# Moving the third transform stage's nine VectorE copies to ScalarE in a fused FFT and two-MLP kernel

## The chip, the cores and the metric

One core of one Trainium2 chip runs the kernel. The metric is the device time of an execution in microseconds (us). Engines are named as in the profile: PE is TensorE's matmul, DVE is VectorE, ACT is ScalarE, POOL is GpSimd, SP is SyncE, which here only issues DMAs.

## What is computed

The reference takes the real part of a two-dimensional FFT of x (2 batches, 3008 rows, 256 features) and sends the 6016 resulting rows through two gated MLPs.

```python
X = np.fft.fft(x, axis=1)
X = np.fft.fft(X, axis=2)
x = X.real.reshape(6016, 256)
gate = 1.0 / (1.0 + np.exp(-(x @ w_gate)))      # 256 -> 1536
x = gate * (x @ w_val) @ w_out                  # 1536 -> 256
h = x @ w_in                                    # 256 -> 2048
out = (h * np.cos(h)) @ w_out2                  # 2048 -> 256
```

The weights arrive as 64-bit floats, and the kernel itself turns them into 32-bit ones.

## The kernel before

The transform over 3008 rows is split into factors 47 and 64, and the one over features is a 128-row cosine or sine matrix. So there are three matmul stages. The first (L325, 16 chunks) writes D1. The second (`stage_b`, L375, 12 calls named b00 to b15) reads D1 and is stored as a rounded high part D2h (ACT, L401) and a remainder D2l (DVE, L405). The third (`stage_c`, L410, six calls c00 to c12, one for each tile of 502 columns) gives three PSUM results a call. These are E (even part), one extra row of features, and O (odd part), and they are copied into the tile's SBUF buffer eo0 to eo5. These 18 copies are the ones in question (L427 on DVE, L430 on ACT). A token is E + O, and its mirror image is E - O.

The first MLP has 6 x 12 = 72 steps (`step1`, L601): one tile by one 128-wide slice of the hidden layer. PE multiplies E into PSUM banks 4 and 5 (`ab(s, 0)`, L475 to L477) and O into banks 6 and 7 (`ab(s, 1)`). DVE adds the extra feature row (`even`, L493, two instructions) and then forms E + O and E - O (`tokens`, L501, two instructions). `ab(s+1, 0)` may not overwrite banks 4 and 5 before L493 of step s has read them, and `ab(s+1, 1)` not banks 6 and 7 before L501 of step s. ACT applies the sigmoid (L649), POOL multiplies gate and value (L505), ACT makes the rounded product and its negative (L589, L590), POOL starts a DMA that adds the exact product onto that negative (L528), and four steps later PE multiplies by the output weights (`out1`, L515 to L518). The second MLP (L539 on) follows.

Beside this, 39 weight units run through a fixed list of steps (`unit_steps`, L139): a DMA into a free buffer, decoding of the 64-bit pattern by two ACT instructions (L118, L119), three DVE instructions (L122, L124, L126) and one POOL instruction (L129), then for most units a rounding on ACT (L134) and a remainder on DVE or POOL (L135); a unit of the first MLP's input weights also has an add and a subtract on DVE or POOL (L150, L151). Their order is fixed when the program is built. The list `clk` holds a planned time for each engine. `regular` (L218) plans a fixed instruction, after `fill` (L196) has placed unit steps that should end before it; `spend` adds its planned length. A step that DVE or POOL may run goes where the planned time is lower. Units whose buffers will be overwritten by the first MLP's own tiles are driven to their end, whatever the planned time, by a loop (L643, L644) that stands just ahead of `tokens(s)` at L646. Each engine then runs its instructions in this order, waiting on semaphores.

The third stage and the first MLP overlap: c10, b15, `ab(0, 0)`, `ab(0, 1)`, c11, `ab(1, 0)`, c12, `ab(1, 1)` is the order on PE. A copy's engine is chosen in `evac` (L421) from the planned times alone.

Of the kernel before, what the change touches and what calls it, by code (L numbers as in the profile page):

```python
# [49 lines left out]
def fft_moe_moe(ctx: ExitStack, tc: tile.TileContext, x, x0, head, w1, w1s, wo1, w2, t1, t3, out):  # L50
# [10 lines left out]
    V, A, G, PE = nc.vector, nc.scalar, nc.gpsimd, nc.tensor  # L61
# [41 lines left out]
    clk = {V: 0.0, A: 0.0, G: 0.0, DQ: 0.0}  # L103
    VG = (V, G)

    def spend(e, us, after=0.0):
        clk[e] = max(clk[e], after) + us
        return clk[e]
# [87 lines left out]
    def fill(e, until):  # L196

        while True:
            for un in live:
                step = un[2][0]  # L200
                if step[0] is VG and e is G and max(un[3], clk[V]) + VADV < max(un[3], clk[G]):
                    continue
                if e in step[0] if step[0] is VG else e is step[0]:
                    if max(un[3], clk[e]) + cost(step, e) <= until:
                        step_of(un, e)
                        break
            else:
                if e is DQ and len(todo) > held[0] and clk[e] + 1.5 <= until:
                    for bf in free:
                        if bf[2] <= until and max(clk[e], bf[2]) + LIFE <= bf[1]:  # L210
                            start(bf)
                            break
                    else:
                        return
                    continue
                return

    def regular(e, us, at=0.0):  # L218

        fill(e, at)  # L220
        return spend(e, us, at)

    def finish(un):
        while un in live:
            step_of(un)
# [46 lines left out]
    def slot(t, us, ahead):  # L272
        while after:
            after.pop(0)()
        for _ in range(2):
            for e, k in zip((DQ, A, G, V), ahead):
                fill(e, t + us + k)
# [93 lines left out]
    def bank():  # L371
        nbank[0] = (nbank[0] + 1) % nbank[1]
        return nbank[0]
# [36 lines left out]
    def stage_c(b, ch, ahead=AHB):  # L410
        slot(now, 2.54, ahead)
        t = b * NCH + ch
        sl = slice(ch * PC, (ch + 1) * PC)
        h0, h1, l0, l1 = D2h[:, 0, sl], D2h[:, 1, sl], D2l[:, 0, sl], D2l[:, 1, sl]

        def mm(terms, dst):
            o = ps[:, bank(), 0:PC]
            for i, (w, m) in enumerate(terms):
                PE.matmul(o, w, m, start=(i == 0), stop=(i == len(terms) - 1))

            def evac(at=now + 2.54):  # L421
                for un in list(live):
                    if un[1] and un[1][0] is flat[t]:
                        finish(un)
                if clk[V] + .59 < clk[A] + .2:
                    regular(V, .59, at)
                    V.tensor_copy(dst, o)  # L427
                else:
                    regular(A, .47, at)
                    A.copy(dst, o)  # L430

            after.append(evac)


        mm([(T3h[:, 0], h0), (T3h[:, 0], l0), (T3l[:, 0], h0), (T3h[:, 2], h1), (T3h[:, 2], l1)],
           eo[t][:, 0, 0:PC])
        mm([(T3h[:, 3], h0), (T3h[:, 3], l0), (T3h[:, 4], h1), (T3h[:, 4], l1)],
           eo[t][:, 0, PC:TW])
        mm([(T3h[:, 1], h1), (T3h[:, 1], l1), (T3l[:, 1], h1)],
           eo[t][:, 1, 0:PC])  # L440
        return now + 2.54
# [364 lines left out]
```

## Time and profile before

| what | value |
|---|---|
| median of 3 runs | 1040.05 us (1039.76 to 1040.32) |
| profiled execution, its own time | 1041.4 us |
| its span, first to last instruction | 1039.5 us |
| mean granted TensorE clock | 0.986 |
| PE busy | 1005.1 us |
| DVE busy | 780.4 us |
| ACT busy | 765.0 us |
| POOL busy | 668.0 us |

A row of a timeline has the start, the length, engine, line, operation, what is written and read, how many instructions are merged, and in brackets the idle time of that engine before it with what ended it. Lengths overlap by some hundredths where the next instruction is started early. The granted clock is the share of full speed, so 0.50 is 1.2 GHz and 1.00 is 2.4 GHz.

### The profile page before, as it was taken

The numbers are of one execution on the slowest core, as the hardware profiler recorded it, in microseconds if no ns is written. First come the engines' busy times: TensorE is split into PE (matmuls) and PEld (weight loads), VectorE is DVE, ScalarE is ACT, GpSimd is POOL, SyncE is SP. The second block draws the span as 40 slices with busy tenths as digits, with TensorE's granted clock in tenths as the row PEclk, the third lists the DMA queues.
The fourth block names the chain that finished last, engine by engine and source line by source line (L and its number), as shares of the span: only waits on it lengthen the run. The fifth ranks groups of instructions, "written<-read, shape, count | busy, mean of one in ns | idle before, by whom it ended". The sixth has DMA issues, their size and how long they took to land.

```text
span 1039.5 us, 13150 instructions
## 1 busy us (share of the span) xinstructions
PE 1005.1 (97%) x4566; PEld 838.0 (81%) x4566; DVE 780.4 (75%) x1033; ACT 765.0 (74%) x1207; POOL 668.0 (64%) x521
## 2 busy tenths in 40 slices
PE   8788899999898999999999999999999999999998
PEld 8776688788786888888788888888888888888886
DVE  3699888877778777777576777777777777777775
ACT  3765566667465567575698888988888888888886
POOL 2685887777676777777365656656566465665753
PEclk9999899999898999999999999999999999999999
DMA  9731556665565566688700000000000000000000
GB/s 255 216 102 41 110 130 140 161 141 124 146 150 121 129 151 146 150 226 211 191 1 20 1 21 0 21 21 1 20 1 21 20 1 21 0 20 21 1 20 21
DMA packets 25955, 85.59 MB, mean 82 GB/s; under 512 B 3168, under 2 KB 6560, under 8 KB 25888
## 3 DMA queue, kind: packets, MB, share of 16 engines
q0 software_dynamic: 10368, 37.02, 19.0%
q1 hardware_dynamic: 15296, 47.59, 14.0%
q8 instruction: 36, 0.59, 0.2%
q14 instruction: 31, 0.25, 0.1%
q10 hardware_dynamic: 224, 0.14, 0.0%
HBM read 33.16 MB, written 14.56 MB: 46 GB/s over the span
## 4 chain that ended last, share of the span: by engine, by line
PE 73%; DVE 4%; ACT 2%; DMA 1%; issue 1%; POOL 0%; DVEq 0%; ACTq 0%
PE ps L557 25%; PE ps L475 12%; PE ps L476 12%; PE ps L477 12%; PE ps L515 4%; PE ps L517 4%; PE ps L518 4%; DVE D L501 3%; DMA gh<-D 1%; ACT gh L589 1%; DVE D L124 1%; DVE D L122 1%; ACT gh L590 1%; DVE D L493 0%; ACT eo L524 0%
## 5 line engine op out<-in xcount | busy, mean ns | idle before, releaser
L583 POOL TENSOR_TENSOR h<-D,h 128x502 fp32r<-128x502 f32 x191 | 284.3, 1489 | 215.8 <-ACT h L582 204.1
L557 PE MATMUL ps<-h,wr 128*128 128x502 f32 x1152 | 291.9, 389 | 0.0
L475 PE MATMUL ps<-es,wr 128*128 128x502 f32 x672 | 265.6, 395 | 16.1 <-DVE D L501 10.9
L476 PE MATMUL ps<-es,wr 128*128 128x502 f32 x672 | 264.3, 393 | 0.0
L477 PE MATMUL ps<-es,wr 128*128 128x502 f32 x672 | 263.3, 392 | 0.0
L557 PEld LDWEIGHTS ps<-h,wr 128*128 128x128 f32 x1152 | 217.8, 189 | 44.4
L505 POOL TENSOR_TENSOR D<-D 128x502 f32<-128x502 f32 x144 | 186.3, 1352 | 93.0 <-ACT D L649 93.0
L568 DVE SCALAR_TENSOR_TENSOR D<-D,ps 128x502 f32<-128x502 int32 x192 | 130.2, 678 | 117.8 <-POOL h L583 110.0
L501 DVE TENSOR_TENSOR D<-D,ps 128x1004 f32<-128x1004 f32 x144 | 172.9, 1201 | 51.6 <-PE ps L477 30.0
L649 ACT ACTIVATE D<-D 128x1004 f32<-128x1004 f32 x72 | 75.1, 1044 | 149.8 <-DVE D L501 149.8
L475 PEld LDWEIGHTS ps<-es,wr 128*128 128x128 f32 x672 | 127.6, 190 | 46.5 <-DVE D L501 13.7
L569 DVE SCALAR_TENSOR_TENSOR D<-D 128x502 f32<-128x502 int32 x192 | 144.8, 754 | 6.6
L477 PEld LDWEIGHTS ps<-es,wr 128*128 128x128 f32 x672 | 127.8, 190 | 26.6
L476 PEld LDWEIGHTS ps<-es,wr 128*128 128x128 f32 x672 | 127.9, 190 | 25.5
L567 ACT ACTIVATE D<-ps 128x502 int32<-128x502 f32 x192 | 113.0, 589 | 47.3 <-PE ps L477 45.4
L575 DVE TENSOR_TENSOR D<-D,ps 128x502 f32<-128x502 f32 x192 | 128.9, 672 | 16.1 <-ACT D L574 16.1
L573 ACT ACTIVATE D<-D 128x502 f32<-128x502 f32 x192 | 119.2, 621 | 12.2 <-DVE D L569 9.7
L493 DVE SCALAR_TENSOR_TENSOR D<-eo,w,ps 128x502 f32<-128x502 f32 x144 | 101.8, 736 | 32.7 <-PE ps L477 32.3
L574 ACT ACTIVATE D<-D 128x502 f32<-128x502 f32 x192 | 120.0, 625 | 6.1
L582 ACT CAST h<-D 128x502 fp32r<-128x502 f32 x192 | 114.6, 597 | 0.2 <-DVE D L575 0.2
L517 PE MATMUL ps<-gh,wr 128*128 128x502 f32 x288 | 114.3, 397 | 0.0
L518 PE MATMUL ps<-gh,wr 128*128 128x502 f32 x288 | 113.4, 394 | 0.0
(86 smaller groups left out, 1073.7 us busy)
## 6 DMA issues: line engine op xcount, KB each, us to landing
gh<-D POOLq DMA_DIRECT2D x72, 502.0 KB, 4.7
D<-in_w_dram SPq DMA_DIRECT2D x17, 512.0 KB, 4.3
ws<-D SPq DMA_DIRECT2D x16, 512.0 KB, 3.6
wr<-ws SPq DMA_DIRECT2D x16, 512.0 KB, 4.0
out_dram<-D SPq DMA_DIRECT2D x24, 251.0 KB, 2.9
raw<-in_x_dram SPq DMA_DIRECT2D x15, 384.0 KB, 9.6
eo<-in_w_dram SPq DMA_DIRECT2D x11, 512.0 KB, 10.3
D<-in_wo_dram SPq DMA_DIRECT2D x6, 512.0 KB, 4.9
```

The costliest lines, as they stand in the source:

```text
L475: PE.matmul(o, w_hi, m_hi, start=first, stop=False)
L476: PE.matmul(o, w_lo, m_hi, start=False, stop=False)
L477: PE.matmul(o, w_hi, m_lo, start=False, stop=last)
L501: V.tensor_tensor(out=gv[s][:, :, c:c + PC], in0=sas, in1=ps[:, 6:8, 0:PC], op=op)
L505: G.tensor_tensor(out=gv[p][:, 1, m], in0=gv[p][:, 1, m], in1=gv[p][:, 0, m], op=ALU.mult)
L517: PE.matmul(o, WO1[:, f, 0, m], h[:, 0, sl], start=(f == 0), stop=False)
L518: PE.matmul(o, WO1[:, f, 1, m], h[:, 0, sl], start=False, stop=False)
L557: PE.matmul(o, WO2[:, f, i, d * 128:(d + 1) * 128], h[:, m], start=(f == 0 and i == m == 0), stop=(f == NF2 - 1 and m == 1))
L568: V.scalar_tensor_tensor(out=r, in0=k, scalar=-C1, in1=h, op0=ALU.mult, op1=ALU.add)
L569: V.scalar_tensor_tensor(out=r, in0=k, scalar=-C2, in1=r, op0=ALU.mult, op1=ALU.add)
L575: V.tensor_tensor(out=r, in0=r, in1=ps[:, 4 + s % 4, 0:PC], op=ALU.mult)
L583: (V if s == N2S - 1 else G).tensor_tensor(out=h[:, 1], in0=r, in1=f32(h[:, 0]), op=ALU.subtract)
```

## The change

All 18 copies are made by ACT, and the planned time of DVE is no longer charged for nine of them.

```diff
@@ stage_c, evac
-                if clk[V] + .59 < clk[A] + .2:
-                    regular(V, .59, at)
-                    V.tensor_copy(dst, o)
-                else:
-                    regular(A, .47, at)
-                    A.copy(dst, o)
+                regular(A, .47, at)
+                A.copy(dst, o)
```

The change shortens the file by four lines, so from there on every line number is four lower in the changed kernel: L493 is L489 there, L501 is L497, L505 is L501, L528 is L524, L589 is L585, L590 is L586, L649 is L645; lines up to L425 keep theirs. As planned times decide the order, steps of weight units move too. D_73 is the buffer of weight units and of the first MLP's tiles, gh the rounded products, wr the finished weights.

POOL from the decoding ahead of the first step's products on. Before:

```order
L129 TENSOR_TENSOR D_73<-D_73 128x512 x2
L505 TENSOR_TENSOR D_73<-D_73 128x502 x2
L528 DMA gh_771<-D_73 128x1004
L505 TENSOR_TENSOR D_73<-D_73 128x502 x4
L528 DMA gh_801<-D_73 128x1004
L505 TENSOR_TENSOR D_73<-D_73 128x502 x2
L528 DMA gh_825<-D_73 128x1004
L135 TENSOR_TENSOR es_770<-eo_66,es_770 128x502
L505 TENSOR_TENSOR D_73<-D_73 128x502 x2
```

and with the change:

```order
L129 TENSOR_TENSOR D_73<-D_73 128x512
L501 TENSOR_TENSOR D_73<-D_73 128x502 x2
L524 DMA gh_769<-D_73 128x1004
L501 TENSOR_TENSOR D_73<-D_73 128x502 x2
L129 TENSOR_TENSOR D_73<-D_73 128x512
L501 TENSOR_TENSOR D_73<-D_73 128x502 x2
L524 DMA gh_802<-D_73 128x1004
L501 TENSOR_TENSOR D_73<-D_73 128x502 x2
L524 DMA gh_826<-D_73 128x1004
L129 TENSOR_TENSOR D_73<-D_73 128x512
L135 TENSOR_TENSOR es_768<-eo_66,es_768 128x502
L501 TENSOR_TENSOR D_73<-D_73 128x502 x2
```

The second of the two L129 that stood together, which belongs to the third output-weight unit, has moved behind the products of step 0, the first product DMA and the products of step 1. Behind the third product DMA there is now an L129 ahead of the next tile's L135 (es).

ACT from the rounding of the second output-weight unit to the second step's product. Before:

```order
L134 CAST wr<-D_73 128x2x256 x2
L118 ACTIVATE D_73<-D_73 128x512
L119 ACTIVATE D_73<-D_73 128x512
L649 ACTIVATE D_73<-D_73 128x1004
L430 COPY eo_70<-ps 128x502
L589 CAST gh_771<-D_73 128x1004
L590 ACTIVATE gh_771<-D_73 128x1004
L649 ACTIVATE D_73<-D_73 128x1004
L589 CAST gh_801<-D_73 128x1004
```

and with the change:

```order
L134 CAST wr<-D_73 128x2x256
L118 ACTIVATE D_73<-D_73 128x512
L119 ACTIVATE D_73<-D_73 128x512
L118 ACTIVATE D_73<-D_73 128x512
L119 ACTIVATE D_73<-D_73 128x512
L645 ACTIVATE D_73<-D_73 128x1004
L426 COPY eo_70<-ps 128x502 x3
L585 CAST gh_769<-D_73 128x1004
L586 ACTIVATE gh_769<-D_73 128x1004
L134 CAST wr<-D_73 128x2x256
L645 ACTIVATE D_73<-D_73 128x1004
L585 CAST gh_802<-D_73 128x1004
```

The sigmoid shown first in each piece is that of step 1. The two L134 of before round the second and the third output-weight unit; the third unit's now stands behind that sigmoid, the three copies of the last tile (one before), and the product pair of step 0.

DVE from the remainder of the third output-weight unit (L135) to `tokens` of step 5. Before:

```order
L135 TENSOR_TENSOR wr<-D_73,wr 128x2x256
L501 TENSOR_TENSOR D_73<-D_73,ps 128x2x502 x2
L493 SCALAR_TENSOR_TENSOR D_73<-eo_65,w_71,ps 128x502 x2
L122 TENSOR_SCALAR D_73<-D_73 128x512
L501 TENSOR_TENSOR D_73<-D_73,ps 128x2x502 x2
L493 SCALAR_TENSOR_TENSOR D_73<-eo_65,w_71,ps 128x502 x2
L124 TENSOR_SCALAR D_73<-D_73 128x512
L501 TENSOR_TENSOR D_73<-D_73,ps 128x2x502 x2
L126 SCALAR_TENSOR_TENSOR D_73<-D_73 128x512
L493 SCALAR_TENSOR_TENSOR D_73<-eo_65,w_71,ps 128x502 x2
L122 TENSOR_SCALAR D_73<-D_73 128x512
L501 TENSOR_TENSOR D_73<-D_73,ps 128x2x502 x2
```

and with the change:

```order
L135 TENSOR_TENSOR wr<-D_73,wr 128x2x256
L497 TENSOR_TENSOR D_73<-D_73,ps 128x2x502 x2
L489 SCALAR_TENSOR_TENSOR D_73<-eo_65,w_71,ps 128x502 x2
L124 TENSOR_SCALAR D_73<-D_73 128x512
L497 TENSOR_TENSOR D_73<-D_73,ps 128x2x502 x2
L489 SCALAR_TENSOR_TENSOR D_73<-eo_65,w_71,ps 128x502 x2
L126 SCALAR_TENSOR_TENSOR D_73<-D_73 128x512
L497 TENSOR_TENSOR D_73<-D_73,ps 128x2x502 x2
L122 TENSOR_SCALAR D_73<-D_73 128x512
L489 SCALAR_TENSOR_TENSOR D_73<-eo_65,w_71,ps 128x502 x2
L124 TENSOR_SCALAR D_73<-D_73 128x512
L497 TENSOR_TENSOR D_73<-D_73,ps 128x2x502 x2
```

The same L135 stands ahead of `tokens(2)`; the decoding steps L122, L124, L126 of the next units have moved, and an L122 now stands right behind `tokens(4)` and ahead of `even(5)`. The matmuls of PE and the DMAs of SP stand in the same order in both kernels.

## Rows read from the trace of the kernel before

**Rows 1.** Waits of PE, whole span: who waited for whom, us in total, times, longest.

```profile
PE ps L475 <- DVE D L501: 10.9, 6, 4.2
```

**Rows 2.** Windows: busy us (instructions) of PE, PEld, DVE, ACT, POOL; granted clock; DMA.

```profile
60.00:92.00 32.00, 27.38 (x159) 23.57 (x158) 31.73 (x49) 19.76 (x44) 27.18 (x22) 0.95 0.15 55
```

**Rows 3.** One line's instructions, L427 and L430: shortest, median, longest ns.

```profile
L427 DVE COPY eo<-ps x9: 664/671/674, 61.3 to 99.5; 128x502 f32<-128x502 f32 x9
...
L430 ACT COPY eo<-ps x9: 552/572/592, 60.2 to 99.9; 128x502 f32<-128x502 f32 x9
```

**Rows 4.** Timeline of DVE from tokens(1) to tokens(3).

```profile
96.51 2.44 DVE L501 TENSOR_TENSOR D<-D,ps 128x1004 f32<-128x1004 f32 x2 [1.41 <-PE ps L477]
...
101.34 0.68 DVE L135 TENSOR_TENSOR wr<-D,wr 128x512 fp32r<-128x512 f32 x1
101.94 2.43 DVE L501 TENSOR_TENSOR D<-D,ps 128x1004 f32<-128x1004 f32 x2
104.47 1.38 DVE L493 SCALAR_TENSOR_TENSOR D<-eo,w,ps 128x502 f32<-128x502 f32 x2
105.77 3.42 DVE L122 TENSOR_SCALAR D<-D 128x512 f32<-128x512 f32 x1
109.11 2.42 DVE L501 TENSOR_TENSOR D<-D,ps 128x1004 f32<-128x1004 f32 x2
```

**Rows 5.** Timeline of ACT: two copies; later the sigmoid of step 1, a product pair.

```profile
66.27 1.02 ACT L430 COPY eo<-ps 128x502 f32<-128x502 f32 x2
...
98.98 1.04 ACT L649 ACTIVATE D<-D 128x1004 f32<-128x1004 f32 x1 [3.62 <-DVE D L501]
...
100.39 1.03 ACT L589 CAST gh<-D 128x1004 fp32r<-128x1004 f32 x1
101.32 1.04 ACT L590 ACTIVATE gh<-D 128x1004 fp32r<-128x1004 f32 x1
```

**Rows 6.** Timeline of POOL: product DMA, four products, a decoding step.

```profile
102.95 1.00 POOL L528 DMA_DIRECT2D gh<-D  x1 [6.72 <-PE ps L477]
103.69 5.21 POOL L505 TENSOR_TENSOR D<-D 128x502 f32<-128x502 f32 x4
...
121.62 1.60 POOL L129 TENSOR_TENSOR D<-D 128x512 int32<-128x512 int32 x1
```

**Rows 7.** Timeline of DVE around 72, 196 and 259 us.

```profile
72.36 1.73 DVE L126 SCALAR_TENSOR_TENSOR D<-D 128x512 uint32<-128x512 uint32 x1
...
195.86 4.58 DVE L124 TENSOR_SCALAR D<-D 128x512 uint32<-128x512 uint32 x1
...
258.61 5.37 DVE L124 TENSOR_SCALAR D<-D 128x512 uint32<-128x512 uint32 x1
```

**Rows 8.** Timeline of POOL around 72 and 259 us.

```profile
72.26 1.28 POOL L135 TENSOR_TENSOR wr<-eo,wr 128x512 fp32r<-128x512 f32 x1 [1.06 <-ACT wr L134]
...
257.62 1.19 POOL L528 DMA_DIRECT2D gh<-D  x1
258.22 1.70 POOL L135 TENSOR_TENSOR es<-eo,es 128x502 fp32r<-128x502 f32 x1
...
260.73 2.87 POOL L505 TENSOR_TENSOR D<-D 128x502 f32<-128x502 f32 x2
```

**Rows 9.** Timeline of PE: the matmuls that waited after the long L124 of 196 and 259 us.

```profile
201.14 0.50 PE L475 MATMUL ps<-es,wr 128*128 128x502 f32 x1 [0.80 <-DVE D L493]
...
204.31 0.50 PE L475 MATMUL ps<-es,wr 128*128 128x502 f32 x1 [1.54 <-DVE D L501]
...
264.68 0.50 PE L475 MATMUL ps<-es,wr 128*128 128x502 f32 x1 [1.34 <-DVE D L493]
...
267.96 0.79 PE L475 MATMUL ps<-es,wr 128*128 128x502 f32 x1 [1.66 <-DVE D L501]
```

**Rows 10.** Windows: two stretches at a granted clock of 0.50, columns as in rows 2.

```profile
109.98:116.81 6.83, 5.22 (x13) 4.18 (x14) 6.30 (x7) 3.40 (x4) 4.05 (x4) 0.50 0.40 78
266.99:273.82 6.83, 5.86 (x14) 4.73 (x15) 5.22 (x6) 3.31 (x4) 4.62 (x4) 0.50 0.45 120
```

## The prediction

> **What bounds the kernel now.** I read the page first, then the waits of PE, then the timelines of all engines from 60 to 140 us, then windows. PE is busy nearly throughout, so only what makes PE wait, or run at half clock, counts. Its largest wait is for L501, `tokens`, on DVE: 10.9 us in six places [rows 1]. The copies in question lie between 60 and 100 us. There DVE is busy 31.73 of 32 us, POOL 27.18, ACT only 19.76 [rows 2]. So DVE looks like the engine to relieve and ACT like the one with room, which speaks for the change. But the order pieces show that more than nine copies moves, and the prediction rests on where three other instructions land.
>
> The reader is to see in [rows 4] that in this part PE follows DVE: `tokens(1)` ends at 98.95, `tokens(2)` starts at 101.94 and `tokens(3)` at 109.11, and each releases PE. The last was late because an L122 took 3.42 us. Such a decoding step is short when POOL is idle, and long when it meets a run of POOL instructions behind a product DMA. The L124 of 258.61 lasted 5.37 us, to 263.98 [rows 7], while POOL worked without a gap from 258.22, right behind L528, until 263.60 [rows 8]. Everything on DVE waits with it.
>
> **The change part by part.** I count from the profiled execution's 1041.4 us (span 1039.5), 1.35 above the median, and carry the difference over to the median, 1040.05. About 0.2%, 2 us, is what a measurement here can tell from no change.
>
> *The copies themselves.* Nine times 0.67 us leave DVE, 6.0 us, and nine times 0.57, 5.1 us, come to ACT [rows 3].
>
> *Term 0: how early `tokens(1)` ends.* Seven of the nine copies stood ahead of it, 4.7 us, and two L135 have gone from there to POOL (the order pieces give them to whichever engine is planned earlier), 0.7 each at the shortest. If all of that came forward, `tokens(1)` would end 6.1 us earlier. I do not take that. DVE's decoding steps in this stretch wait for POOL, not for DVE: the L126 of 72.36 ended at 74.09, 0.55 after the POOL instruction that ended at 73.54 [rows 7, 8], and POOL has little idle time [rows 2]. The copies read PSUM and ran while POOL worked, so that without them DVE reaches the next decoding step earlier and waits there. POOL, with two L135 more at about 1.28 and one L151 less, can even push DVE back by some 2 us. The stall of `stage_c` for D2l may shrink, but PE then reaches `ab(1, 0)` sooner and waits for DVE there. I take 0, with ends of -6.1 and +2.1, because [rows 2] put POOL nearest to full beside DVE.
>
> *Term 1: the new wait ahead of `tokens(2)`.* The third output-weight unit is driven to its end by the loop of L643 before `tokens(2)`. Its remainder L135 needs its rounding L134 on ACT, which needs its L129 on POOL. Before, that L129 ran early, and the L135 of 101.34 waited for nothing [rows 4]. Now POOL has the L129 behind the first product DMA and the products of step 1; that DMA waits for L590 of step 0; and on ACT that stands behind the sigmoid of step 1 and three copies; and the sigmoid waits for `tokens(1)`. From the end of `tokens(1)` the chain is: sigmoid 0.95 to the next start, three copies 1.4 (two take 1.02), L589 0.93, L590 1.04 [rows 5]; product DMA 0.74 to the next start, two L505 at 5.21/4, 2.6 [rows 6]; L129 1.5 of the 1.60 that a row shows [rows 6]; L134 about 0.6, as a copy; L135 0.60 to the next start [rows 4]. That makes 10.4 us less some early starts, 10.2. Before, the gap was 101.94 - 98.95 = 3.0. So `tokens(2)` comes 7.2 us later. Behind this L135 stand all of DVE's queue and, through it, PE's `ab(3, 1)`. Nothing covers it: PE has only `ab(3, 0)` left. PE falls to half clock after it, but it did so after the old wait too: 0.50 from 109.98 to 116.81 with 5.22 us busy [rows 10], so the clock's price is in both.
>
> *Term 2: the old stall goes.* Ahead of `tokens(3)` stands an L124 now, not that L122, and POOL is no longer in a long run then, for its products of step 2 wait for the sigmoid behind `tokens(2)`. From the end of `tokens(2)` to `tokens(3)` it was 109.11 - 104.37 = 4.7 us [rows 4]; now two L493, 1.38, and an L124 that waits for one product at most, 1.3 + 0.2, give 2.9. That gives back 1.8.
>
> *Term 3: a new stall behind `tokens(4)`.* An L122 stands there now, ahead of `even(5)`. By its place POOL has just issued the third product DMA and has, in one run behind it, an L129, the next tile's L135 and two products: 1.5 + 1.28 + 2.6 = 5.4 us [rows 6, 8], of which I reckon that DVE meets the last 4 to 5. This is the pattern of 195.86 and 258.61. There the price was 0.80 + 1.54 = 2.3 us of waits, and 1.34 + 1.66 = 3.0 of waits plus half of the 5.86 us busy at half clock, 2.9, together 5.9 [rows 9, 10]. I take 5, near the dearer, because here too an L124 follows between `even(5)` and `tokens(5)`. The ends are 0 and 5.9.
>
> The Trainium skill, SBUF — State Buffer, section Who interferes with whom, says that GpSimd and certain VectorE instructions take a shared port pair one whole instruction at a time, and that the second to issue blocks until the first finishes. By that rule an L122 would lose one POOL instruction, about 1.3 us, and term 3 would be hidden by PE's own work: 1045, the first rival below. The rows of 195.86 and 258.61 speak against it, with 4.6 and 5.4 us.
>
> The Trainium skill, TensorEngine Tiling (Array Packing), section PSUM Bottleneck, speaks against the change: it advises to use both ScalarE and VectorE to empty PSUM. By that rule alone the loss is the copies' 5.1 us on ACT, 1045; by rows 2 ACT has 12 us to spare there.
>
> The sum: 0 + 7.2 - 1.8 + 5.0 = 10.4. Beyond 186 us the order is the same on every engine, and PE sets the pace before that, so the stalls of 196 and 259 us and a third at 325 should come again. 1040.05 + 10.4 = 1050.4; I say 1050.
>
> **The rivals.**
>
> *No second stall.* Term 3 is 0, as POOL leaves a gap when the L122 comes: 1040.05 + 5.4 = 1045. For it: the L126 of 72.36 got in between two POOL instructions [rows 7, 8]. Against: the run behind the DMA has no instruction that waits for something late. Chance 0.25.
>
> *The relief counts in full.* Term 0 is -6.1, and no second stall: 1040.05 - 6.1 + 5.4 = 1039, no difference to be seen. For it: DVE is 99% busy in [rows 2]. Against: POOL's 27.18 there. Chance 0.08.
>
> *Faster: the later stalls vanish.* With POOL's work in another phase, the long L124 of 196 and 259 us and the like at 325 find POOL idle: 2.3 + 5.9 + 5.9 = 14.1 less, 1036. It decides when all three go, or two without the second stall. Against: the order there is unchanged. Chance 0.06.
>
> *One stall more.* Between 125 and 186 us the decoding steps also stand differently, and one more L122 or L124 can meet a POOL run: 1050 + 5.9 = 1056. Chance 0.07.
>
> That the change does not do what it says is excluded: DVE's pieces have no copy of this stage left.
>
> **How the numbers follow.** The forecast has 0.54. Likeliest time: 1050. Its own range, from term 0 at -3 to +2.1 and term 3 up to 5.9, is 1047 to 1053.5. To hold 8 in 10 the range takes in the first rival's 1045 with term 0 at -3, so 1042, and reaches to 1055; outside lie 1039, 1036 and most of 1056. Faster by over 0.2%: 0.06. Within 0.2%: 0.08. Slower: 0.86.
>
> **What would show it.** Right: `tokens(1)` ends near 99; L135 ahead of `tokens(2)` is preceded by 7 to 8 us of idle DVE with ACT's L134 as releaser, and before that ACT waits for POOL's L129; PE waits 8 us or more for `tokens(2)`; near 123 us an L122 of over 4 us and a PE wait behind it; PE's matmuls between 140 and 180 us are 10 us later than before. Wrong: if `tokens(1)` ends at 95 or earlier, term 0 failed; if the L135 waits less than 4 us, term 1; if that L122 is under 1.5 us, term 3; if the PE waits near 196, 259 and 325 us are gone, the claim about the later part.

## The result and the profile after

| | before | changed |
|---|---|---|
| median of 6 runs | 1040.19 us (1039.76 to 1043.32) | 1050.58 us (1048.00 to 1052.57) |
| profiled execution, its own time | 1041.4 us | 1052.57 us |
| span | 1039.5 us | 1050.8 us |
| ratio of the runs | | 1.0081, 95% interval 1.0061 to 1.0102 |

The change makes the kernel 0.8% slower, at the forecast 1050. The profiled execution of the changed kernel is 11.2 us longer than that of before, and PE's waits for DVE are the first place to look. The waits of PE after the change, who waited for whom, with us in total, times, and the longest:

```profile
PE ps L471 <- DVE D L497: 16.6, 7, 10.4
PE ps L471 <- DVE D L489: 9.5, 4, 4.3
```

The first row answers to [rows 1]: 10.9 us in six places with a longest of 4.2 have become 16.6 in seven with one of 10.4. The timelines tell which place that is. DVE after the change, from `tokens(1)` to `tokens(5)` (L497), answers to [rows 4]:

```profile
96.08 2.44 DVE L497 TENSOR_TENSOR D<-D,ps 128x1004 f32<-128x1004 f32 x2 [2.22 <-PE ps L473]
...
99.92 0.42 DVE L122 TENSOR_SCALAR D<-D 128x512 f32<-128x512 f32 x1
108.87 0.69 DVE L135 TENSOR_TENSOR wr<-D,wr 128x512 fp32r<-128x512 f32 x1 [8.53 <-ACT wr L134]
109.48 2.43 DVE L497 TENSOR_TENSOR D<-D,ps 128x1004 f32<-128x1004 f32 x2
...
113.31 1.30 DVE L124 TENSOR_SCALAR D<-D 128x512 uint32<-128x512 uint32 x1
114.88 2.43 DVE L497 TENSOR_TENSOR D<-D,ps 128x1004 f32<-128x1004 f32 x2 [0.27 <-PE ps L473]
...
120.28 2.42 DVE L497 TENSOR_TENSOR D<-D,ps 128x1004 f32<-128x1004 f32 x2
122.61 8.15 DVE L122 TENSOR_SCALAR D<-D 128x512 f32<-128x512 f32 x1
...
132.32 2.42 DVE L497 TENSOR_TENSOR D<-D,ps 128x1004 f32<-128x1004 f32 x2
```

Two rows hold the loss: the L135 of 108.87 behind 8.53 us of idle DVE, and the L122 of 122.61, which took 8.15 us where the L122 of 99.92 took 0.42. Whom the first one waited for is seen on ACT and POOL. ACT:

```profile
98.55 1.04 ACT L645 ACTIVATE D<-D 128x1004 f32<-128x1004 f32 x1 [3.60 <-DVE D L497]
99.50 1.52 ACT L426 COPY eo<-ps 128x502 f32<-128x502 f32 x3
100.89 1.05 ACT L585 CAST gh<-D 128x1004 fp32r<-128x1004 f32 x1
101.82 1.06 ACT L586 ACTIVATE gh<-D 128x1004 fp32r<-128x1004 f32 x1
108.22 0.62 ACT L134 CAST wr<-D 128x512 fp32r<-128x512 f32 x1 [5.33 <-POOL D L129]
```

POOL in the same stretch, and behind the third product DMA (L524):

```profile
103.48 1.00 POOL L524 DMA_DIRECT2D gh<-D  x1 [10.17 <-ACT gh L586]
104.22 2.73 POOL L501 TENSOR_TENSOR D<-D 128x502 f32<-128x502 f32 x2
106.62 1.56 POOL L129 TENSOR_TENSOR D<-D 128x512 int32<-128x512 int32 x1
...
121.43 0.86 POOL L524 DMA_DIRECT2D gh<-D  x1
122.04 1.61 POOL L129 TENSOR_TENSOR D<-D 128x512 int32<-128x512 int32 x1
123.30 1.57 POOL L135 TENSOR_TENSOR es<-eo,es 128x502 fp32r<-128x502 f32 x1
124.53 2.78 POOL L501 TENSOR_TENSOR D<-D 128x502 f32<-128x502 f32 x2
126.98 1.17 POOL L524 DMA_DIRECT2D gh<-D  x1
127.59 1.86 POOL L135 TENSOR_TENSOR wr<-D,wr 128x512 fp32r<-128x512 f32 x1
128.81 1.66 POOL L135 TENSOR_TENSOR es<-eo,es 128x502 fp32r<-128x502 f32 x1
```

The chain of term 1 can be read from link to link: end of `tokens(1)` 98.52, sigmoid, three copies, L585 and L586 to 102.88, DMA, two products, L129 to 108.18, L134 to 108.84, L135. Then the L122 of 122.61 ends at 130.76, 0.29 after POOL's run ended at 130.47: it waited for everything that POOL had lined up, two further L135 and a second DMA (126.98) among it. PE, the matmuls that waited between 100 and 140 us:

```profile
111.96 0.79 PE L471 MATMUL ps<-es,wr 128*128 128x502 f32 x1 [10.37 <-DVE D L497]
117.36 0.49 PE L471 MATMUL ps<-es,wr 128*128 128x502 f32 x1 [0.56 <-DVE D L497]
131.47 0.79 PE L471 MATMUL ps<-es,wr 128*128 128x502 f32 x1 [4.28 <-DVE D L489]
134.80 0.79 PE L471 MATMUL ps<-es,wr 128*128 128x502 f32 x1 [0.45 <-DVE D L497]
```

Windows of three stretches after the change (columns as in [rows 2]): the one of the copies, and two at a granted clock of 0.50, 1.2 GHz:

```profile
60.00:92.00 32.00, 27.63 (x160) 23.17 (x159) 30.57 (x43) 21.62 (x48) 27.77 (x23) 1.00 0.12 44
```

```profile
105.80:116.04 10.24, 4.08 (x10) 3.30 (x11) 6.76 (x7) 3.52 (x4) 5.37 (x5) 0.50 0.18 33
129.69:136.52 6.83, 4.60 (x10) 3.28 (x11) 6.69 (x9) 1.74 (x2) 1.41 (x2) 0.50 0.23 43
```

### The profile page after: what moved, and what is told of

It reads as the page before. It is cut to its first block, busy times and chain, and to the rows that moved or that the text cites. A ratio compares the mean times of both kernels' runs of the same rounds, so it can differ in the third digit from the quotient of the medians.

```text
span 1050.8 us, 13147 instructions
## 1 busy us (share of the span) xinstructions
PE 1008.4 (96%) x4566; PEld 838.8 (80%) x4566; DVE 781.7 (74%) x1023; ACT 768.8 (73%) x1216; POOL 669.9 (64%) x522
## 4 chain that ended last, share of the span: by engine, by line
PE 78%; DVE 5%; ACT 2%; issue 2%; DMA 1%; POOL 0%; DVEq 0%; ACTq 0%
PE ps L553 25%; PE ps L471 13%; PE ps L472 13%; PE ps L473 13%; PE ps L513 5%; PE ps L511 5%; PE ps L514 5%; DVE D L497 3%; DVE D L122 1%; DMA gh<-D 1%; DVE D L124 1%; ACT gh L585 1%; ACT gh L586 1%; DVE D L489 1%; ACT eo L520 0%
## 5 line engine op out<-in xcount | busy, mean ns | idle before, releaser
L471 PE MATMUL ps<-es,wr 128*128 128x502 f32 x672 | 267.1, 397 | 26.0 <-DVE D L497 16.6
L501 POOL TENSOR_TENSOR D<-D 128x502 f32<-128x502 f32 x144 | 186.6, 1347 | 101.4 <-ACT D L645 100.2
L497 DVE TENSOR_TENSOR D<-D,ps 128x1004 f32<-128x1004 f32 x144 | 172.8, 1200 | 51.6 <-PE ps L473 31.7
L645 ACT ACTIVATE D<-D 128x1004 f32<-128x1004 f32 x72 | 75.1, 1044 | 162.2 <-DVE D L497 162.2
L489 DVE SCALAR_TENSOR_TENSOR D<-eo,w,ps 128x502 f32<-128x502 f32 x144 | 101.7, 735 | 33.5 <-PE ps L473 32.8
```

The source lines that it names most:

```text
L471: PE.matmul(o, w_hi, m_hi, start=first, stop=False)
L497: V.tensor_tensor(out=gv[s][:, :, c:c + PC], in0=sas, in1=ps[:, 6:8, 0:PC], op=op)
L501: G.tensor_tensor(out=gv[p][:, 1, m], in0=gv[p][:, 1, m], in1=gv[p][:, 0, m], op=ALU.mult)
```

## The experiments

The theory to be tested: the copies cost and gain nothing; the loss is in the order that the planned times give, as a new wait ahead of `tokens(2)` and a long L122 behind `tokens(4)`. On the three chips of the experiments the kernel before took between 1038.3 and 1049.2 us, with a median of 1043.4 on each, so what counts is the ratio to before, measured on the same chip, with its 95% interval. A per cent is 10.4 us. Where an edit adds lines, the line numbers behind it are higher by as many. "Lined up matmul by matmul" means: PE's matmuls stand in the same order in every kernel, so each can be compared with the same one in another trace, and the difference of their starts tells how far PE is behind there.

### The copies alone and the order alone

One kernel has the order of before with all copies on ACT:

```diff
@@ evac, of the kernel before
                 if clk[V] + .59 < clk[A] + .2:
                     regular(V, .59, at)
-                    V.tensor_copy(dst, o)
                 else:
                     regular(A, .47, at)
-                    A.copy(dst, o)
+                A.copy(dst, o)
```

> Edit: the planned times are charged as in the kernel before, so every other instruction stands where it stood there, but all 18 copies are issued on ACT. Theory (the loss comes from the order that the planned times give, not from the copies): 1040 us, within 2 us of the kernel before, 1040.2; tokens(2) starts 3 us after the end of tokens(1), the L122 ahead of tokens(3) lasts over 3 us again, and there is no DVE instruction of 8 us near 123 us. Rival 1 (ACT was the better place for none of the nine: their 5.1 us delay the rounding and the sigmoid): 1045. Rival 2 (the copies off DVE are a gain that the new order hides): 1037 or less, with tokens(1) ending at 95 or earlier.

The other has the changed kernel's order with the nine copies back on DVE (k is which of the tile's three results it is):

```diff
@@ evac, of the changed kernel
                 regular(A, .47, at)
-                A.copy(dst, o)
+                if (t, k) in ((0, 1), (1, 1), (2, 0), (2, 2), (4, 0), (4, 1), (4, 2), (5, 0), (5, 1)):
+                    V.tensor_copy(dst, o)
+                else:
+                    A.copy(dst, o)
```

> Edit: the planned times and so the order are those of the changed kernel, but the nine copies that VectorE made before are issued on DVE again. Theory (order alone): 1050 to 1052 us; the idle time of DVE ahead of tokens(2) is 7 to 9 us with ACT's L134 as releaser, and an L122 behind tokens(4) lasts 6 us or more. Rival (the copies on ACT are the loss): 1040 to 1042, with ACT's chain between tokens(1) and L134 shorter by two copies, 1 us. If both count, between, about 1046.

The copies alone: ratio 0.9986 (0.9964 to 1.0007), median 1041.12. The order alone: 1.0073 (1.0046 to 1.0101), median 1051.0. So the loss belongs to the order, and the rival that ACT's copies cost 5 us falls. That they hide a gain has no support either: in the first kernel's trace `tokens(1)` ends at 100.23, not at 95 or earlier. DVE with the order alone shows both marks:

```profile
109.45 0.69 DVE L135 TENSOR_TENSOR wr<-D,wr 128x512 fp32r<-128x512 f32 x1 [6.58 <-ACT wr L134]
...
123.20 8.16 DVE L122 TENSOR_SCALAR D<-D 128x512 f32<-128x512 f32 x1
```

The wait of 6.58 is below the 7 to 9 expected: two copies fewer stand in ACT's chain and two more on DVE.

One thing went against the expectation of the first kernel. Its profiled execution took 1048.81, 7.7 above its median, and holds a long step near 123 after all, though the order is that of before:

```profile
106.07 5.33 DVE L122 TENSOR_SCALAR D<-D 128x512 f32<-128x512 f32 x1
...
124.88 6.43 DVE L124 TENSOR_SCALAR D<-D 128x512 uint32<-128x512 uint32 x1
```

In the profile of before the same L122 took 3.42 [rows 4], and no step near 124 was long. So one order can have this stall or not, by some us of phase between DVE and POOL. That this is why the kernel before itself spreads over 10 us was not shown; one profile of each kernel is all there is.

### Undoing the two places one at a time

The wait ahead of `tokens(2)`: the third output-weight unit's L129 and L134 are issued early, and all else stays (its L126, issued in the same loop, keeps its place on DVE).

```diff
@@ step1, of the changed kernel
             ahead(G, gate_at)
+            if s == 1:
+                for un in live:
+                    if un[0] == ("wo1", 2):
+                        for k in (0, 1, 2):
+                            e, us, issue = un[2][k]
+                            issue()
+                            un[2][k] = (e, us, lambda: None)
             for c in (0, PC):
                 times(s - 1, c)
```

> Edit to the changed kernel: the L129 of the third output-weight unit is issued on POOL ahead of the products of step 0, and its L134 on ACT right behind the second unit's, as before the change; nothing else moves on any engine. Theory (the wait ahead of tokens(2) is worth its 8 us and the L122 behind tokens(4) is a loss of its own): tokens(2) starts 3 us after the end of tokens(1), the L122 behind tokens(4) lasts over 4 us all the same, and the time is 1042 to 1044. Rival 1 (the long L122 exists only because the wait shifts POOL against DVE): both go, 1035 to 1037. Rival 2 (what is gained ahead of tokens(2) is lost to another wait): 1049 to 1051.

Ratio 1.0039 (1.0018 to 1.0060), median 1047.6, so 0.0042 or 4.4 us below the changed kernel. DVE:

```profile
99.65 2.43 DVE L497 TENSOR_TENSOR D<-D,ps 128x1004 f32<-128x1004 f32 x2
...
103.49 4.97 DVE L124 TENSOR_SCALAR D<-D 128x512 uint32<-128x512 uint32 x1
...
116.29 7.98 DVE L122 TENSOR_SCALAR D<-D 128x512 f32<-128x512 f32 x1
```

`tokens(2)` now starts 2.3 us after the end of `tokens(1)`, 97.31, as the theory said, and the long L122 is there without the wait: it is a loss of its own, and the first rival falls. But the whole 8 us did not come back, because the old stall ahead of `tokens(3)` returned, as an L124 of 4.97. So terms 1 and 2 of the prediction cannot be undone one without the other: together they brought 4.4 us here, and 0.39%, 4 us, is left to before, for term 3 and the rest.

The long L122: it and the L124 behind it are issued behind `tokens(5)`.

```diff
@@ step_of, of the changed kernel
-            step[2]()
+            if put[0] and e is V:
+                put[1].append(step[2])
+            else:
+                step[2]()
@@ step1
+            put[0] = s == 5
             ahead(V, now + 3 * MM)
             even(s)
...
             tokens(s)
+            put[0] = False
+            while put[1]:
+                put[1].pop(0)()
```

> Edit to the changed kernel: the L122 behind tokens(4) and the L124 behind even(5) are both issued right behind tokens(5); nothing else moves. Theory (the long L122 is a loss of its own, some 7 us, because even(5) and tokens(5) stand behind it): even(5) and tokens(5) follow tokens(4) without a gap and the 4.3 us wait of PE for L489 near 131 us goes; the L122 behind tokens(5) may still be long, but has ab(6) beside it, so that it costs at most 3: 1043 to 1047. Rival (the wait ahead of tokens(2) causes all of the loss, and PE would have stood still at this place anyway): 1050 to 1051.

Ratio 1.0076 (1.0048 to 1.0104): nothing gained, the rival's number. DVE and then PE show that it is not for the rival's reason:

```profile
123.36 2.44 DVE L501 TENSOR_TENSOR D<-D,ps 128x1004 f32<-128x1004 f32 x2 [0.34 <-PE ps L477]
125.71 6.37 DVE L122 TENSOR_SCALAR D<-D 128x512 f32<-128x512 f32 x1
```

```profile
133.27 0.49 PE L475 MATMUL ps<-es,wr 128*128 128x502 f32 x1 [1.83 <-DVE D L493]
136.87 0.79 PE L475 MATMUL ps<-es,wr 128*128 128x502 f32 x1 [1.98 <-DVE D L501]
```

`tokens(5)` (L501 here) did come early, 26.0 us after the end of `tokens(1)` (97.33 there) in place of 33.8. But POOL was still in the same run, without a gap from 117.4 to 132.7, the L122 waited in it until 132.08, and `even(6)` (L493) and `tokens(6)` stood behind it. The stall moved by one step.

So the two steps were issued earlier instead, right behind `tokens(3)`, where POOL stands idle:

```diff
@@ step1, of the changed kernel
             tokens(s)
+            if s == 3:
+                for un in live:
+                    if un[0] == ("wo1", 4):
+                        for k in (0, 1):
+                            e, us, issue = un[2][k]
+                            issue()
+                            un[2][k] = (e, us, lambda: None)
```

> Edit to the changed kernel: the L122 behind tokens(4) and the L124 behind even(5), of the fifth output-weight unit, are both issued right behind tokens(3); nothing else moves. In the changed kernel's trace POOL stands idle there from 116.5 to 118.5 us. Theory (a decoding step of this kind is dear only where a run of POOL instructions stands beside it, so that it can be placed at no cost): both take under 0.6 us, PE's wait near 131 us goes, and the kernel takes 7 us less than the changed one, some 1043 where before takes 1040. Rival (moving it only moves the stall, as when it was issued behind tokens(5)): a long step of 4 us or more stands within 10 us of the place, and the time stays at 1050.

Ratio 1.0055 (1.0031 to 1.0079), median 1049.3, 2.7 us below the changed kernel, with intervals that overlap: between theory and rival. DVE:

```profile
115.70 0.42 DVE L122 TENSOR_SCALAR D<-D 128x512 f32<-128x512 f32 x1
116.16 0.43 DVE L124 TENSOR_SCALAR D<-D 128x512 uint32<-128x512 uint32 x1
...
127.75 4.25 DVE L126 SCALAR_TENSOR_TENSOR D<-D 128x512 uint32<-128x512 uint32 x1
```

Both took what they take alone, as the theory said. Lined up matmul by matmul, PE gains 7.3 us on the changed kernel's trace around 131 us, and that is what the long L122 was worth. But the unit's third step, L126, now met the POOL run behind a DMA and took 4.25, and 3.7 us were lost again. I had held that an L126, with two inputs, is never long. That fell here.

### Is it the form of the instruction?

The three kernels of this group were made on that belief. L122 and L124 become instructions of L126's form, with the second number read from SBUF, first in the changed kernel:

```diff
@@ dec_steps
-            (V, .34, lambda: V.tensor_scalar(out=t, in0=t, scalar1=FMIN, scalar2=FMAX,
-                                             op0=ALU.max, op1=ALU.min)),
-            (V, .34, lambda: V.tensor_scalar(out=u, in0=u, scalar1=3, scalar2=0x7FFFFFFF,
-                                             op0=ALU.logical_shift_left, op1=ALU.bitwise_and)),
+            (V, .34, lambda: V.scalar_tensor_tensor(out=t, in0=t, scalar=FMIN, in1=fmax.to_broadcast([128, n]),
+                                                    op0=ALU.max, op1=ALU.min)),
+            (V, .34, lambda: V.scalar_tensor_tensor(out=u, in0=u, scalar=3, in1=mask.to_broadcast([128, n]),
+                                                    op0=ALU.logical_shift_left, op1=ALU.bitwise_and)),
```

> Edit to the changed kernel: L122 and L124 keep their place and their values but are scalar_tensor_tensor instructions that read the second number from a constant column of SBUF, the form of L126, which took at most 1.78 us in both traces. Theory (the long waits belong to the one-input form with two immediate numbers, whose VectorE instruction waits for a whole run of POOL): no L122 or L124 over 2.5 us, the PE waits near 131, 196 to 206, 259 to 268 and 325 to 334 us go, the wait ahead of tokens(2) stays: 1050.5 - 7 - 12 = 1031, ends 1027 to 1036. Rival (any VectorE instruction between SBUF operands waits for POOL's run, and L126 merely stood at better places): 4 to 8 us at the same places, 1050 or, with each step 0.3 us longer, up to 1056.

Then with the early L129 and L134 besides:

> Edit to the changed kernel: the two-input form of L122 and L124, and the L129 of the third output-weight unit ahead of the products of step 0 with its L134 behind the second unit's. Theory: the wait ahead of tokens(2) goes as well, 8 us less than with the two-input form alone, and the stall ahead of tokens(3) does not come back, since its L124 is of the two-input form: 1023 to 1027. Rival (the stall ahead of tokens(3) comes back): 1028 to 1030.

And alone, in the kernel before:

> Edit to the kernel before: the two-input form of L122 and L124 alone. Theory: its four long steps go, 1.8 + 2.3 + 5.9 + 5.9 = 16 us at most: 1024 to 1030, and within 2 us of the changed kernel with the two-input form and the early L129: the order that the copies' planned times give is then worth nothing either way. Rival (the copies on ACT pay once the stalls are gone, because DVE's longer decoding steps make it the bound in the stretch of 60 to 100 us): this one 3 us or more slower than that one.

All three are slower than before, where 1023 to 1036 us was forecast: 1.0167 (1.0136 to 1.0199), 1.0110 (1.0080 to 1.0139) and 1.0045 (1.0015 to 1.0075). The step behind `tokens(4)` in the first of them (its L124 is the old L122):

```profile
132.03 8.41 DVE L124 SCALAR_TENSOR_TENSOR D<-D,consts 128x512 f32<-128x512 f32 x1
```

8.41 us with two inputs against 8.15 with one: the form makes no difference to the wait. A step of the longer form takes at least 0.69 where the old L122 takes 0.42, and PE is late already ahead of `tokens(1)`: lined up matmul by matmul, it is 9.0, 8.3 and 7.3 us behind before's trace at 98 us, more than half of it by 60 us. The last of the three, in the order of before, is the fastest, so nothing shows that copies on ACT pay with DVE's steps made longer.

### Is it the DMA at the head of POOL's run?

Every long step so far stood in a run of POOL that began with, or held, a product DMA. So each product DMA was put at the end of its run: held back, and issued behind the unit steps, ahead of the next products.

```diff
@@ lo1, of the changed kernel
-        G.dma_start(out=f32(gh[p][:, 1]), in_=gv[p][:, 1], accum_op=ALU.add)
+        out, src = f32(gh[p][:, 1]), gv[p][:, 1]
+        held_lo.append(lambda: G.dma_start(out=out, in_=src, accum_op=ALU.add))
@@ step1
             ahead(G, gate_at)
+            while held_lo:
+                held_lo.pop(0)()
             for c in (0, PC):
                 times(s - 1, c)
                 done[s - 1] = spend(G, 1.3, gate_at) + .1
+        while s > N1S and held_lo:
+            held_lo.pop(0)()
```

> Edit to the changed kernel: each product DMA on POOL is issued behind the unit steps that follow it, ahead of the next step's products, instead of ahead of those steps; the other engines' order is the same. In all traces so far a VectorE instruction between SBUF operands that meets a POOL run with no DMA in it took at most 1.94 us, and all of over 2 us met a run behind a DMA. Theory (it is the DMA at the head of the run that makes VectorE wait for the whole run): the L122 behind tokens(4) takes under 2 us and PE's wait of 4 us near 131 goes; most of those near 205, 268 and 334 us go too; 1050.5 - 7 = 1043 at the least, 1030 if all go. Rival (the run's length alone decides): 6 to 8 us at the same L122 and 1050.

Ratio 1.0004 (0.9988 to 1.0020): as fast as before. This does not mean that the loss of the change is undone, for the kernel before gains by the same edit too (0.9949, below), and against that the changed kernel is still 0.55% slower. DVE, POOL (L525 is the product DMA here) and PE near the place:

```profile
122.39 0.43 DVE L122 TENSOR_SCALAR D<-D 128x512 f32<-128x512 f32 x1
...
124.04 5.82 DVE L124 TENSOR_SCALAR D<-D 128x512 uint32<-128x512 uint32 x1
```

```profile
121.23 1.30 POOL L129 TENSOR_TENSOR D<-D 128x512 int32<-128x512 int32 x1
122.49 1.46 POOL L135 TENSOR_TENSOR es<-eo,es 128x502 fp32r<-128x502 f32 x1
123.90 0.86 POOL L525 DMA_DIRECT2D gh<-D  x1
124.50 2.80 POOL L501 TENSOR_TENSOR D<-D 128x502 f32<-128x502 f32 x2
126.97 1.57 POOL L135 TENSOR_TENSOR wr<-D,wr 128x512 fp32r<-128x512 f32 x1
128.22 1.35 POOL L135 TENSOR_TENSOR es<-eo,es 128x502 fp32r<-128x502 f32 x1
```

```profile
132.26 0.58 PE L471 MATMUL ps<-es,wr 128*128 128x502 f32 x1 [3.91 <-DVE D L497]
```

These rows show both cases within two microseconds. The L122 stands beside the same L129 and L135 as in the changed kernel, but no DMA is ahead of them, and it takes 0.43 in place of 8.15. The L124 of 124.04 starts 0.14 behind the start of the DMA and takes 5.82, to 0.29 behind the L135 that ends at 129.57, after which POOL issues its next DMA. So the stall near `tokens(5)` was made smaller, not removed: PE still waits 3.91 us, and, lined up matmul by matmul, loses 5.7 us there in place of 7.3. At 140 us it is 8.9 us behind before's trace, in place of 10.7. Most of the gain comes from later, where the long step near 334 is gone, a stall that the kernel before has too, and PE gets 6 us back; an L122 near 266 still takes 6.2.

The same edit in the kernel before, and with the early L129 and L134 in the changed kernel:

> Edit to the kernel before: the product DMA behind the unit steps, as in the run above. Theory: the long steps near 106, 196, 259 and 325 us go, and with them up to 14 to 16 us: 1025 to 1032 against 1040 to 1043. Rival (the run's length decides, or the products come too late for the output matmuls four steps on): 1040 or more.

> Edit to the changed kernel: the product DMA behind the unit steps, and the L129 and L134 of the third output-weight unit early. Theory: both new waits of the change go, and the old stalls: the same as the kernel before with the DMA behind, within 2 us, 1025 to 1032. Rival (the copies on ACT are worth something once the stalls are gone): 3 us or more below that one.

Ratios 0.9949 (0.9937 to 0.9961) and 0.9938 (0.9922 to 0.9954), medians 1037.7 and 1036.1: both beat the kernel before and the changed one, but before by only 5 to 7 us and not the 10 and more expected. Long steps are left near 104 to 107, 196 and 257 to 260, where POOL is late and the products themselves follow a DMA without a gap. The two do not differ by what these intervals can tell, so the rival, that the copies pay once the stalls are gone, is not shown. The early L129 and L134 took the changed kernel from 1.0004 to 0.9938 here, 0.66% or 6.9 us, which is all that was left of the change's loss: in this trace the wait ahead of `tokens(2)` is gone, and near `tokens(5)` L122 and L124 take 1.44 and 1.00.

## Why the prediction was right, point by point

*The copies.* Right. They are worth nothing that can be told from no change: 0.9986 with an interval that holds 1. Between 60 and 92 us DVE was rid of 3.2 us of them, yet its busy time fell from 31.73 [rows 2] to 30.57 only. With the copies alone moved, one can see where the time went: from 62 us to `tokens(1)` DVE's other instructions, the same as before, took 34.7 us together in place of 32.3, and nearly all of the difference lies in those that work in SBUF alone (23.4 against 21.0). The advice of the Trainium skill, TensorEngine Tiling (Array Packing), section PSUM Bottleneck, to use both engines, would have made the copies alone slower; the runs show no difference (0.9986).

*Term 0*, 0 us. Right as a number, and partly by luck: `tokens(1)` ends at 98.52 against 98.95 [rows 4], but as the sum of a gain and a loss of 5 us each. Before, PE waited 3.76 us for D2l and then ran at half clock until 82.67; after, the waits for D2l are 1.17 and 0.37, and lined up matmul by matmul PE is 5.4 us ahead near 90 us. It gives that back by a wait of 0.87 for `even(0)`, one of 1.96 for a copy on ACT, which stands behind the first sigmoid, and a half-clock stretch of 3.41 us in which it is busy throughout, half of which, 1.7, is lost. The first row is from before, the others from after:

```profile
79.47 0.79 PE L419 MATMUL ps<-D2l,T3h 128*128 128x502 f32 x1 [3.76 <-DVE D2l L405]
```

```profile
91.26 0.49 PE L419 MATMUL ps<-D2h,T3h 128*128 128x502 f32 x1 [1.96 <-ACT eo L426]
```

```profile
92.15:95.56 3.41, 3.41 (x10) 2.71 (x9) 1.15 (x1) 2.80 (x6) 1.16 (x1) 0.50 0.00 0
```

The prediction named the shorter stall of `stage_c` and the wait for DVE behind it. It did not name the copy on ACT and the clock, and POOL, its reason for taking 0, explains only why DVE's own steps did not get shorter.

*Term 1*, +7.2. Right in every link, and 0.8 short: from the end of `tokens(1)` to `tokens(2)` it is 109.48 - 98.52 = 10.96, in place of 10.2, against 3.0 before, +8.0. The difference is the handing over between engines, which was not counted: 0.60 lies between the end of L586 at 102.88 and the start of the DMA at 103.48. The three copies were as reckoned.

*Term 2*, -1.8. Right: from the end of `tokens(2)`, 111.91, to `tokens(3)`, 114.88, it is 2.97 against 4.74. The three terms make +5.8 at `tokens(3)`, where +5.4 was forecast.

*"The clock's price is in both."* Wrong, and in the change's favour. Before, PE went on from the wait for `tokens(3)` at half clock until 116.81, 5.22 us busy [rows 10]. After, the half-clock stretch is longer, 105.80 to 116.04, but its 4.08 busy us lie ahead of the next wait for DVE, of which 0.56 is left at 117.36; what the clock took there PE would have waited anyway. Lined up matmul by matmul, PE is 5.8 us behind before's trace as it leaves `tokens(3)` and 3.4 behind near 118 us: 2.4 given back.

*Term 3*, +5, ends 0 to 5.9. The place and the pattern were right, the size was not, and it lies above the upper end. Priced like 259 us, it is 4.28 + 0.45 of waits and half of 4.60 busy, 2.3: 7.0. Matmul by matmul PE goes from 3.4 to 10.7 behind, 7.3. The step that failed is the length of POOL's run, "an L129, the next tile's L135 and two products": the run did not end there but took in the next product DMA and two more L135, so DVE waited 8.15 us rather than 4 to 5.

*Later.* Right in the main: the stalls near 196, 259 and 325 came again, as L122 of 4.16 at 205, L124 of 5.38 at 268 and L122 of 5.44 at 334, and from 140 us to the end PE stays 9.6 to 11.5 us behind. So 1050 was met partly because 0.8 + 2.3 too little and 2.4 too much cancel, as do the two parts of term 0.

*The rivals.* No second stall (1045) fell with the L122 of 122.61, the relief in full (1039) with `tokens(1)` at 98.52, faster (1036) with the long steps at 205, 268 and 334. One stall more (1056) did not come: PE's lag of 10.7 us does not grow from 130 to 180 us. The Trainium skill's rule in SBUF — State Buffer, section Who interferes with whom, that the second to issue is blocked for one whole instruction, agrees with POOL's runs without a DMA, where no VectorE instruction took over 1.94 us; behind a DMA it does not, with up to 8.41 (below).

## What to carry to other kernels

Where planned times set the order, a cheaper instruction also moves whatever the planner put around it: compare the order of all engines, and price the two or three instructions that land elsewhere before the copies themselves. Look at what a moved step waits for through other engines, and at what stands behind it in its own queue. And an instruction on VectorE that works in SBUF alone has no fixed price beside GpSimd: see whether a DMA issued by GpSimd stands in the run that it meets, and try that DMA behind the work, not ahead of it; in the kernel before that alone brought 0.5%.

## What the hardware showed that was not expected

I counted VectorE's instructions from 60 us on in all thirteen traces, by what GpSimd did when they started (a run is GpSimd work, DMA issues included, without a gap of 0.12 us). Of instructions with all operands in SBUF that met a run without a DMA so far, 489, the longest took 1.94 us. That the run's length decides is refuted by this group: 236 of them met a run that went on for 3 us or more. Of those that met a run in which a DMA had been issued and more work followed, 85, 52 took over 2 us, up to 8.41; 30 of the other 33 had started within 0.25 us of the start of the DMA issue. Of the instructions with an operand in PSUM that met GpSimd at work, 4985, none took over 1.20. Outside the second group no instruction took over 2 us.

The 52 did not wait until GpSimd was idle as a rule. 43 ended while GpSimd's next DMA issue was under way, 3 just behind one, and 6 with GpSimd idle. The L122 of 122.61 is one of the 6: the DMA issue of 126.98 came and went, and it waited on.

That a DMA ahead in the run makes the difference is shown by these counts and by the L122 of the changed kernel with the DMA behind, 0.43 us beside the same work. Why it does, and why some DMA issues end the wait and others do not, was not tried and stays open. The form of VectorE's instruction (one input or two) has no part in it: 8.15 and 8.41 us.

A second surprise was how small a shift between engines decides. In the same order one L122 took 3.42 us in one execution and 5.33 in another with the copies moved, and in the latter an L124 then met a second run 19 us later and took 6.43.
